# Seven products for eight in the first gate chunk, sums of w_down on Pool, gated loads, last store by ACT

## The chip, the cores and the metric

The kernel runs on one core of one Trainium2 chip. Times are device microseconds (us) of that core. The engines are PE (TensorE), PEld (its weight loads), DVE (VectorE), ACT (ScalarE), POOL (GpSimd, "Pool") and SP (SyncE, which only issues DMAs here). A traced execution has a "span" some 2 us shorter than the timed one. Traces are compared by spans, kernels by times. A single run of a one-core program has no known state, and is called a single run below.

## The reference, cut to what matters

```python
def _B_ref(x, w_gate, w_up, w_down):                 # x: 2048 x 448, F = 1792
    return (_gelu(x @ w_gate) * (x @ w_up)) @ w_down
x = A_x
xn = _layernorm(x)
s = attention(xn, k_cache, v_cache, wq, wo)          # 16 heads of 256, the last 512 keys  (cut)
g = silu(_B_ref(xn, w_gate, w_up, w_down))
return x + s * g
```

The 2048 rows go in four chunks of 512. The gate of a chunk is one matrix product with `w_down` (1792 x 448) after the gelu and the multiplication.

## The kernel before: the parts that matter

The program is a list of operations. Each goes to the in-order queue of one engine, and a semaphore wait is put in wherever an operation needs another engine's result. So an operation that is late makes everything behind it on its engine late (in experiment 12 a dead VectorE subtraction of 5.72 us made the multiplication behind it 5.07 us late).

TensorE forms gate and up for 128 columns at a time (a "unit"), two units per "pair", 28 pairs for the four chunks. After each unit ACT takes the gelu and VectorE multiplies:

```python
def gu_evac(n, b):
    act(gl[:, s, :], bank[b], ACT.Gelu_apprx_tanh, ...)
    o = actTh if c else actT                 # first chunk: bf16; later ones: f16
    K.op("dve", lambda e: e.tensor_tensor(o[:, c % 2, f, :], bank[b + 1], gl[:, s, :], ALU.mult), ...)
```

The pair after next fills the same banks again, so TensorE stops if VectorE is late with a multiplication (6.0 us of such waits in the trace of the changed kernel).

The product with `w_down` exists in two forms. `down` is the plain one, for the first chunk: 4 row tiles x 14 matmuls of 448 columns in bf16. `down7` cuts both operands in 2 x 2 blocks and needs seven block products for eight, in f16, for sums of activations (`sum_act`) and of weights (`sum_wd`) formed beforehand:

```python
def sum_wd(o, x, y):                         # 128 x 1568, f16
    add("dve", wdt[o][0], wdt[x][0], wdt[y][0], ..., ALU.subtract)
def sum_act(c, k, i=None):                   # 128 x 1024 or 128 x 768, f16
    ...
    add("dve", S(j)[0], x, y, bx + by, S(j)[1], op)
...
for n in range(4, NU, 2):                    # one unit pair
    gu_group((n, n + 1), cur)
    gu_evac(n, cur[0]); ln_b(); gu_evac(n + 1, cur[1])     # ln_b: normalisation of one tile of 128 rows
    if ln_t[0] < 8 or n >= 12: ln_a()                      # ln_a: its statistics, on VectorE and Pool
    ...                                                    # casts, sums: some per pair
    if n + 1 in DOWN_AT:                                   # {NF + 5: 0, 39: 1}
        ...                                                # down(0) after pair 18, down7(1) after pair 38
```

Attention follows: scores, softmax, a DMA transpose of the softmax weights (`pT<-pn`, 128 of them), the product with V, and `w_o`. Some gates of g and rows of x are loaded again through Pool's DMA queue.

The softmax here doesn't subtract the row's maximum and nothing guards it: scores larger than these inputs give would overflow.

## Time and profile before

| | before |
|---|---|
| time, first three runs | 543.99 us (543.13 to 544.43) |
| traced span | 541.5 us |
| PE / DVE / ACT / POOL busy | 535.7 / 376.3 / 313.4 / 39.5 us |
| mean granted TensorE clock | 0.999 |

TensorE is busy for 99% of the span, so it is the bound, and VectorE for 69%. The lines of the profile are in the prediction.

### The profile page before, as it was taken

What the parts mean: (1) busy time and instruction counts of PE and PEld (TensorE: products, weight loads), DVE (VectorE), ACT (ScalarE), POOL (GpSimd) and SP (SyncE); (2) the same over time, 40 slices, a digit from 0 to 9 for tenths busy, and PEclk for the clock granted to TensorE, in tenths of its full rate; (3) what the DMA queues carried; (4) which work ended last, traced back from release to release, by engine and by line L of the source; (5) the groups of instructions that cost most, each with busy time, mean ns of one, the idle gap of its engine ahead of it and who ended that gap; (6) DMA issues with size and microseconds to landing.
All of it is one profiled execution on the core that took longest, in us unless ns stands there. A gap on an engine that the chain in (4) does not pass through costs nothing.

```text
span 541.5 us, 10848 instructions
## 1 busy us (share of the span) xinstructions
PE 535.7 (99%) x4138; PEld 306.3 (57%) x4138; DVE 376.3 (69%) x825; ACT 313.4 (58%) x780; POOL 39.5 (7%) x78
## 2 busy tenths in 40 slices
PE   8999999999999999999999999999999999999997
PEld 5554457449644444884444469544444984444587
DVE  6673885799767757934875786467667934776775
ACT  5433854873667858206875860388488216876820
POOL 1130400000002000003001000120100003001010
PEclk9999999999999999999999999999999999999999
DMA  9569261921487767302781670066457402873731
GB/s 298 120 186 130 45 142 41 301 64 42 113 189 159 157 145 149 77 1 69 164 156 45 148 146 1 18 142 153 96 105 150 67 1 72 167 151 82 135 71 35
DMA packets 171604, 61.38 MB, mean 113 GB/s; under 512 B 155104, under 2 KB 168416, under 8 KB 171552
## 3 DMA queue, kind: packets, MB, share of 16 engines
q1 hardware_dynamic: 167776, 51.39, 43.7%
q0 software_dynamic: 3008, 8.72, 6.9%
q8 instruction: 33, 0.54, 0.4%
q10 hardware_dynamic: 768, 0.57, 0.3%
q14 instruction: 19, 0.16, 0.1%
HBM read 19.76 MB, written 3.67 MB: 43 GB/s over the span
## 4 chain that ended last, share of the span: by engine, by line
PE 97%; DMA 1%; DVE 0%; issue 0%; ACT 0%; ACTq 0%
PE bank L392 97%; DMA pT<-pn 1%; DMA x<-in_A_x_dram 0%; DVE stats L439 0%; PE bank L490 0%; DVE xn L465 0%; DVE mv L442 0%; ACT p L844 0%; PE bank L509 0%; DVE xnT L898 0%; DVE xnT L386 0%; DVE rstd L459 0%; ACTq L155 0%
## 5 line engine op out<-in xcount | busy, mean ns | idle before, releaser
L844 ACT ACTIVATE p<-bank 128x512 f32<-128x512 f32 x256 | 150.6, 596 | 28.2 <-DVE pn L851 26.4
L392 PE MATMUL bank<-pT,va 128*128 128x512 bf16 x512 | 120.8, 379 | 1.0 <-DMA pT<-pn 1.0
L392 PE MATMUL bank<-kT,qT 128*128 128x512 bf16 x512 | 121.0, 379 | 0.0
L851 DVE TENSOR_SCALAR pn<-p,rden 128x512 bf16<-128x512 f32 x256 | 113.0, 484 | 8.2 <-DMA pT<-pn 3.9
L392 PE MATMUL bank<-xnT,wq 64*128 64x512 bf16 x768 | 94.9, 376 | 0.0
L392 PEld LDWEIGHTS bank<-pT,va 128*128 128x128 bf16 x512 | 49.9, 98 | 61.5 <-DMA pT<-pn 2.2
L392 PEld LDWEIGHTS bank<-kT,qT 128*128 128x128 bf16 x512 | 49.4, 98 | 61.7 <-issue 3.4
L392 PE MATMUL bank<-xnT,wgu 64*128 64x512 bf16 (+2 forms) x768 | 83.9, 350 | 0.1
L383 ACT ACTIVATE qT<-bank 128x512 bf16<-128x512 f32 x76 | 44.1, 596 | 51.9 <-PE bank L392 50.3
L829 DVE CAST qT<-bank 128x512 bf16<-128x512 f32 x52 | 34.9, 690 | 49.6 <-PE bank L392 49.6
L392 PEld LDWEIGHTS bank<-xnT,wq 64*128 64x128 bf16 x768 | 36.7, 94 | 46.3 <-ACT p L844 2.1
L392 PEld LDWEIGHTS bank<-xnT,wgu 64*128 64x128 bf16 x768 | 36.9, 94 | 36.8 <-issue 0.6
L848 DVE RECIPROCAL rden<-rsum 128x2 f32<-128x2 f32 x128 | 21.2, 165 | 47.4 <-ACT p L844 47.2
L844 ACT ACTIVATION_READ_ACCUMULATOR p<-bank 128x1 f32 x256 | 51.6, 202 | 0.0
L392 PE MATMUL bank<-wt,sr 128*128 128x224 f16 x512 | 50.0, 259 | 0.0
L383 ACT ACTIVATE gl<-bank 128x512 bf16<-128x512 f32 x56 | 33.1, 596 | 28.5 <-PE bank L392 26.1
L392 PEld LDWEIGHTS bank<-wt,sr 128*128 128x128 f16 x512 | 49.0, 98 | 0.4 <-ACT oTh L383 0.2
L869 DVE TENSOR_SCALAR oTh<-bank 128x512 f16<-128x512 f32 x62 | 42.4, 684 | 0.0
L383 ACT ACTIVATE oTh<-bank 128x512 f16<-128x512 f32 x66 | 38.9, 590 | 4.1 <-PE bank L392 4.1
L392 PE MATMUL bank<-wt,oTh 128*128 128x224 f16 (+1 forms) x416 | 38.4, 252 | 0.0
L392 PEld LDWEIGHTS bank<-wt,oTh 128*128 128x128 f16 x416 | 37.2, 98 | 0.9
L377 POOL DMA_DIRECT2D g<-g_all x14 | 7.8, 556 | 379.9 <-DVE xnT L386 285.0
(82 smaller groups left out, 403.7 us busy)
## 6 DMA issues: line engine op xcount, KB each, us to landing
wtb<-in_A_wo_dram POOLq DMA_DIRECT2D x4, 896.0 KB, 10.4
wq<-in_A_wq_dram SPq DMA_DIRECT2D x2, 1536.0 KB, 7.2
va<-in_A_v_cache_dram SPq DMA_DIRECT2D x8, 256.0 KB, 5.2
pT<-pn SPq DMA_TRANSPOSE x128, 2.7
xr<-in_A_x_dram POOLq DMA_DIRECT2D x15, 112.0 KB, 2.4
wd<-in_B_w_down_dram SPq DMA_DIRECT2D x1, 1568.0 KB, 7.9
g<-g_all POOLq DMA_DIRECT2D x14, 112.0 KB, 2.3
out_dram<-xr POOLq DMA_DIRECT2D x12, 112.0 KB, 2.2
```

Of the source, the lines that this page charges most:

```text
L377: K.op(q, lambda e, o=o, i=i: e.dma_start(o, i), reads, writes, dma=True)
L383: K.op("act", lambda e, o=o, i=i: e.activation(o, i, func, scale=scale), reads, writes)
L392: ins = e.matmul(o, lhsT=l, rhs=r, start=st, stop=sp, skip_group_check=True)
L829: K.op("dve", lambda v, s=s, b=b: v.tensor_copy(qT[:, s, 1, :], bank[b + 1]), (b_ps[b + 1],), (b_qT[s][1],))
L844: K.op("act", lambda e, b=b, r=r, z=z: e.activation(p32[:, z, :], bank[b], ACT.Exp, scale=att_scale, accum_out=rsum[:, r:r + 1]), (b_ps[b] ...
L848: K.op("dve", lambda e, r=r: e.reciprocal(rden[:, r - 1:r + 1], rsum[:, r - 1:r + 1]), b_rsum[r - 1:r + 1], b_rden[r - 1:r + 1])
L851: K.op("dve", lambda e, r=r - 1 + t, z=(n - 1 + t) % NP32, y=y, t=t: e.tensor_scalar(pn[:, y, t, :], p32[:, z, :], rden[:, r:r + 1], None, ...
L869: K.op("dve", lambda v, i=i, b=b: v.tensor_scalar(oTh[:, i, :], bank[b], WS, None, op0=ALU.mult), (b_ps[b],), (b_oT[i],))
```

## The change

The intent is to save TensorE time in the first chunk (98 half-width matmuls for 56), to give Pool, idle for 93% of the span, the sums of weights, to move layer norms out of the pairs in which these sums run, and to remove two small waits in attention and at the end.

```diff
+        dn[0] = (dict(dn[1][0]),) + dn[1][1:]              # same places for the sums of chunk 0
-            o = actTh if c else actT                       # gu_evac: f16 always
-        def down(c, pairs): ...                            (removed)
         def sum_wd(o, x, y):
-            add("dve", wdt[o][0], wdt[x][0], wdt[y][0], ..., ALU.subtract)
+            add("pool", wdt[o][0], wdt[x][0], wdt[y][0], ..., ALU.subtract)
-        WD_CASTS = [(20, ...                               # casts of w_down by ACT
+        WD_CASTS = [(16, ...
-        DN_SUMS = [(24, sum_act, (1, k, 0)) ...] + [(30, sum_wd, x) ...] + [(34, sum_act, (1, k, 1)) ...]
+        WD_SUMS = [(20, (4, 4, 0)), (22, (5, 2, 4)), (22, (6, 5, 0)), (24, (3, 1, 5))]
+        ACT_SUMS = [(n, (c, k, i)) for c, i, ns in ((0, 0, (10, 10, 20, 20)), (0, 1, (22, 22, 24, 24)), ...
-        DOWN_AT = {NF + 5: 0, 39: 1}
+        DOWN_AT = {27: 0, 39: 1}
-            if ln_t[0] < 8 or n >= 12:
+            if ln_t[0] < 8 or 12 <= n and ln_t[0] < 12 or n >= 28:
+                def norms():                               # two layer norms, within down7 of chunk 0
+                    for f in (ln_a, ln_a, ln_b, ln_b): f()
-            dma("sp", out_view[:, t, c0:c1], ...)          # last_end
+            dma("sp" if c1 < N2 else "act", out_view[:, t, c0:c1], ...)
+                        now = [[o for o in K.ops if o.eng == "pe"][-1]]
-                            load_g2(t)                     # and the loads of xr likewise
+                            load_g2(t, now)                # not before TensorE has come to this place
... (cuts within and between the parts)
```

More of the change, by code (lines that the diff above doesn't have):

```diff
@@ L334, in bass_recurrent_scan__sliding_block_cached__geglu_ffn__prompt_kernel @@
                         [a_wq + 3 * SD + (3 + i) * CD for i in range(2)])}
+        dn[0] = (dict(dn[1][0]),) + dn[1][1:]
+        dn[0][0][3] = (actTh[:, 0, 0:NH, HC:QC], b_actT[0][0:NH])
         NPT, NPN, NP32 = 3, 3, 3
@@ L373, in qs, with dma @@
             return n - g + (QS - Q0 if g == 0 else 0)
-        def dma(q, o, i, reads=(), writes=()):
-            K.op(q, lambda e, o=o, i=i: e.dma_start(o, i), reads, writes, dma=True)
+        def dma(q, o, i, reads=(), writes=(), after=()):
+            K.op(q, lambda e, o=o, i=i: e.dma_start(o, i), reads, writes, dma=True, after=after)
         def dma_t(o, i, reads=(), writes=()):
@@ L557, in gu_evac @@
             act(gl[:, s, :], bank[b], ACT.Gelu_apprx_tanh, (b_ps[b],), (b_gl[s],))
-            o = actTh if c else actT
-            K.op("dve", lambda e: e.tensor_tensor(o[:, c % 2, f, :], bank[b + 1], gl[:, s, :], ALU.mult),
+            K.op("dve", lambda e: e.tensor_tensor(actTh[:, c % 2, f, :], bank[b + 1], gl[:, s, :], ALU.mult),
                  (b_ps[b + 1], b_gl[s]), (b_actT[c % 2][f],))
-        def down(c, pairs):
-            for t4 in range(4):
-                t = c * 4 + t4
-                b = bk(pairs, t4)
-                mms([(bank[b][:, 0:D], actT[:, c % 2, f, t4 * P:(t4 + 1) * P], wd[:, f, :], f == 0, f == NF - 1)
-                     for f in range(NF)], [b_wd] + b_actT[c % 2], (b_ps[b],))
-                s = t % 2
-                act(tmp[:, s, 0:D], bank[b][:, 0:D], ACT.Tanh, (b_ps[b],), (b_tmp[s],), scale=0.5)
-                K.op("dve", lambda e, t4=t4, b=b, s=s: e.scalar_tensor_tensor(
-                    out=g2w[t4 // 2][:, t4 % 2, :], in0=tmp[:, s, 0:D], scalar=1.0, in1=bank[b][:, 0:D],
-                    op0=ALU.add, op1=ALU.mult), (b_tmp[s], b_ps[b]), (b_g2w[t4],))
-                dma("sp", g2d[t], g2w[t4 // 2][:, t4 % 2, :], (b_g2w[t4],), (b_g2d[t],))
         def cast_wd(j, e, n, i):
@@ L581, in sum_wd @@
         def sum_wd(o, x, y):
-            add("dve", wdt[o][0], wdt[x][0], wdt[y][0], [wdt[x][1], wdt[y][1]], [wdt[o][1]], ALU.subtract)
+            add("pool", wdt[o][0], wdt[x][0], wdt[y][0], [wdt[x][1], wdt[y][1]], [wdt[o][1]], ALU.subtract)
         def sum_act(c, k, i=None):
@@ L750, in bass_recurrent_scan__sliding_block_cached__geglu_ffn__prompt_kernel @@
             (48, (o, x, y, i)) for i in range(NB) for o, x, y in ((5, 2, 4), (6, 5, 0), (3, 1, 5))]
-        WD_CASTS = [(20, (j, e, n, i)) for j, e, n in ((0, 0, 0), (4, 0, 1), (2, 1, 1), (1, 1, 0)) for i in range(2)]
-        DN_SUMS = [(24, sum_act, (1, k, 0)) for k in range(4)] + [
-            (30, sum_wd, x) for x in ((4, 4, 0), (5, 2, 4), (6, 5, 0), (3, 1, 5))] + [(34, sum_act, (1, k, 1)) for k in range(4)]
-        DOWN_AT = {NF + 5: 0, 39: 1}
+        WD_CASTS = [(16, (j, e, n, i)) for j, e, n in ((0, 0, 0), (4, 0, 1), (2, 1, 1), (1, 1, 0)) for i in range(2)]
+        WD_SUMS = [(20, (4, 4, 0)), (22, (5, 2, 4)), (22, (6, 5, 0)), (24, (3, 1, 5))]
+        ACT_SUMS = [(n, (c, k, i)) for c, i, ns in ((0, 0, (10, 10, 20, 20)), (0, 1, (22, 22, 24, 24)),
+                                                    (1, 0, (30, 32, 34, 34)), (1, 1, (36, 36, 38, 38)))
+                    for k, n in enumerate(ns)]
+        DOWN_AT = {27: 0, 39: 1}
         gu_evac(0, 0)
@@ L780, in bass_recurrent_scan__sliding_block_cached__geglu_ffn__prompt_kernel @@
                 load_wt(1, 1, 0)
-            for i in range(2 if n >= 24 else 1):
+            for i in range(2):
                 if WD_CASTS and n >= WD_CASTS[0][0]:
                     cast_wd(*WD_CASTS.pop(0)[1])
-            for i in range(2 if n in (30, 32, 34, 36) else 1):
-                if DN_SUMS and n >= DN_SUMS[0][0]:
-                    _, f, x = DN_SUMS.pop(0)
-                    f(*x)
+            while WD_SUMS and n >= WD_SUMS[0][0]:
+                sum_wd(*WD_SUMS.pop(0)[1])
+            while ACT_SUMS and n >= ACT_SUMS[0][0]:
+                sum_act(*ACT_SUMS.pop(0)[1])
             for i in range(2 if n >= 40 else 1):
@@ L794, in bass_recurrent_scan__sliding_block_cached__geglu_ffn__prompt_kernel @@
             if n + 1 in DOWN_AT:
-                assert not DN_SUMS or DN_SUMS[0][0] > n, DN_SUMS
-                if DOWN_AT[n + 1] == 1:
-                    end = down7(1, (cur[0], cur[0] + 1, cur[1], cur[1] + 1, nxt[0], nxt[0] + 1),
-                          (g2x[:, 0:2, :], g2x[:, 2:4, :]), b_g2x)
-                    end(0, 1)
-                    end(2, 3)
-                    cur, nxt = (nxt[1], cur[1]), (cur[0], nxt[0])
-                else:
-                    down(DOWN_AT[n + 1], cur)
-                    cur, nxt = nxt, cur
-                    K.reuse([wdt[j][1] for j in (0, 1, 2, 4)])
+                def norms():
+                    for f in (ln_a, ln_a, ln_b, ln_b):
+                        f()
+                end = down7(DOWN_AT[n + 1], (cur[0], cur[0] + 1, cur[1], cur[1] + 1, nxt[0], nxt[0] + 1),
+                            (g2x[:, 0:2, :], g2x[:, 2:4, :]), b_g2x, then=norms if n < 28 else None)
+                end(0, 1)
+                end(2, 3)
+                cur, nxt = (nxt[1], cur[1]), (cur[0], nxt[0])
                 if DOWN_AT[n + 1] == 1:
@@ L873, in bass_recurrent_scan__sliding_block_cached__geglu_ffn__prompt_kernel, with load_g2 @@
         o_view = oTh.rearrange("p (h e) (r q) -> p e r h q", e=2, r=2)
-        def load_g2(t):
-            dma("pool", g2[:, t % NG2, :], g2d[t], (b_g2d[t],), (b_g2[t % NG2],))
+        def load_g2(t, after=()):
+            dma("pool", g2[:, t % NG2, :], g2d[t], (b_g2d[t],), (b_g2[t % NG2],), after)
         def burst_end(t, ns=(0, 1)):
@@ L900, in last_end @@
             add("dve", xs[:, t4, c0:c1], xs[:, t4, c0:c1], x[:, c0:c1], by + bx, by)
-            dma("sp", out_view[:, t, c0:c1], xs[:, t4, c0:c1], by, ())
+            dma("sp" if c1 < N2 else "act", out_view[:, t, c0:c1], xs[:, t4, c0:c1], by, ())
         def burst(c):
@@ L1035, in bass_recurrent_scan__sliding_block_cached__geglu_ffn__prompt_kernel @@
                             load_v(g)
+                        now = [[o for o in K.ops if o.eng == "pe"][-1]]
                         for t in range(NG2):
-                            load_g2(t)
+                            load_g2(t, now)
                         for t in range(NXR):
-                            dma("pool", xr[:, t, :], x_view[:, t, :], (), b_xr[t])
+                            dma("pool", xr[:, t, :], x_view[:, t, :], (), b_xr[t], now)
                     if end and p:
```

## The prediction

> **What bounds the kernel now.** I read the page's busy table and the slices first, then the chain that ended last, then the waits of TensorE, then the timelines of TensorE, Pool and the store queue in the stretches that the change touches.
>
> ```profile
> PE 535.7 (99%) x4138; PEld 306.3 (57%) x4138; DVE 376.3 (69%) x825; ACT 313.4 (58%) x780; POOL 39.5 (7%) x78
> PE 97%; DMA 1%; DVE 0%; issue 0%; ACT 0%; ACTq 0%
> ```
>
> TensorE (PE) works 535.7 of 541.5 us at the full granted clock, and 97% of the chain that ended last is its matmuls. So only three things can move the time: less TensorE work, fewer TensorE waits, a shorter tail. The waits of TensorE are three lines in all:
>
> ```profile
> PE bank L509 <- DVE epst L423: 1.2, 1, 1.2
> PE bank L392 <- DMA pT<-pn: 1.0, 1, 1.0
> PE bank L490 <- DVE xn L465: 0.4, 1, 0.4
> ```
>
> The first and third are the start, which the change leaves alone. The second is one wait inside attention, at 170 us; the chain in order of time shows it:
>
> ```profile
> 164.73 5.29 DMA pT<-pn
> 170.02 0.05 issue
> 170.07 368.31 PE bank L392 x2592
> ```
>
> One transpose of softmax weights took 5.29 us to land, where the page's list of DMA issues has 2.7 us as the median of these 128. Beside it the Pool timeline has this:
>
> ```profile
> 162.59 1.32 POOL L377 DMA_DIRECT2D g<-g_all  x2 [94.99 <-DVE rden L848]
> 163.90 1.59 POOL L377 DMA_DIRECT2D xr<-in_A_x_dram  x3
> ```
>
> Five loads of 112 KB each, issued just before that transpose. These are the loads the change gates.
>
> [...] a VectorE sum ran from 60.42 to 61.08, and the small Pool operation that began at 60.59 took 0.56 us, to 61.15, where its like at 57.57 took 0.22:
>
> ```profile
> 57.57 0.22 POOL L449 TENSOR_SCALAR ve<-mv 128x1 f32<-128x1 f32 x1 [2.15 <-DVE mv L442]
> 60.59 0.56 POOL L449 TENSOR_SCALAR ve<-mv 128x1 f32<-128x1 f32 x1 [2.15 <-DVE mv L442]
> ```
>
> [...]
>
> **The change, part by part.**
>
> *Seven products for eight, first chunk.* The old form and the form that the second chunk already uses stand in the TensorE timeline:
>
> ```profile
> 37.92 10.77 PE L392 MATMUL bank<-wd,actT 128*128 128x448 bf16 x56
> 48.62 0.82 PE L392 MATMUL bank<-xnT,wgu 64*128 64x512 bf16 x6
> ...
> 78.94 1.51 PE L392 MATMUL bank<-wdh,actTh 128*128 128x224 f16 x14
> ...
> 88.44 0.82 PE L392 MATMUL bank<-xnT,wgu 64*128 64x512 bf16 x6
> ```
>
> Start to start, the old form takes 48.62 - 37.92 = 10.70 us (56 x 191 ns), the new one 88.44 - 78.94 = 9.50 us (98 x 96.9 ns). Saved on the path: **1.20 us**. The products move from after unit pair 18 to after unit pair 26, which costs TensorE nothing.
>
> *Sums of activations.* Eight more on VectorE: four of 1024 elements at 0.66 to 0.68 us and four of 768 at 0.55 us, together 4.9 us. One pair of units lasts 3.02 us (gelus start at 34.35 and 37.37). In the pairs 20 to 26 VectorE has two multiplications, about 1.3 us, and, as the layer norms are moved out, at most 1.3 us of sums (pair 20 also still has one normalisation, 0.6 us): 3.2 us in pair 20, 2.4 us in 22 and 24. Nothing is lost, if these run at their present durations.
>
> *Sums of w_down to Pool.* VectorE is freed of four of 1568 elements, 0.96 to 0.97 us each, 3.9 us in all; off the path before, so no gain. On Pool they get a deadline. The products now start at 37.92 + 4 x 3.02 = 50.0 us. The first product (9.50/7 = 1.36 us) needs no sum; the second, from 51.36 us, reads the sum that Pool forms last. Pool can start when its last reciprocal root is done, 41.42 + 0.57 = 42.0 us (the casts on ACT are done earlier: after the gelus of pair 18 at 38.5, plus 1.74 us, so 40.3). So it has **9.36 us for four sums, 2.34 us each.** [...]
>
> *Layer norms of two tiles within the products.* About 2.9 us of VectorE (twice 0.62 + 0.18 for the statistics, 0.6 for the normalisation) at the start of a 9.5 us stage in which VectorE otherwise waits (3.6 us for TensorE before its first combination in the second chunk). Hidden, though their Pool steps queue behind the sums.
>
> *Gated loads.* Five loads leave 162.6 us and are issued after the first query projection of the next group, about 192 us. The transposes at 163 to 170 us keep the engines to themselves, so the wait of **1.03 us** should go. At 192 us they meet two K transposes and three V loads; the DMA is already about full from 193 to 199 us. 0.56 MB at some 250 GB/s adds an estimated 2.2 us there. K must be there at 198.3, the first V at 200.1 us; the V loads are issued at 194.1 us and take 4.4 us, so land at about 199. There is 1 to 2 us of slack: a stall of 0 to 1 us is possible.
>
> *Last store by ACT.* The store queue's timeline around the three last stores:
>
> ```profile
> 537.67 0.33 SPq L377 DMA_DIRECT2D out_dram<-xnT  x1
> 538.16 1.17 SPq L377 DMA_DIRECT2D out_dram<-xnT  x1
> ```
>
> The second issue held the queue until 539.33, while the last result was ready at 538.71 + 0.22 = 538.93. From ACT's own queue it can go at once: **0.4 us** off the tail.
>
> *Sum.* 543.99 - 1.20 - 1.03 - 0.4 = 541.4 us, before whatever Pool costs.
>
> **The rivals.**
> *A: Pool is in time.* Speaking for it is the shape of the change: casts are moved four units earlier, layer norms are moved out of exactly the pairs in which Pool sums, and the products are put off to pair 26. That looks like a schedule fitted to a slow Pool. Time: 541.2 to 541.8 us.
> *B: Pool is late.* The sums end after 51.36 us and a new wait of TensorE for Pool takes the place of what was saved. [...]
> *C: Pool locks out VectorE.* The six activation sums in pairs 20 to 24 each wait for a Pool sum, and Pool for them (six times 0.6 us, 3.7 us more for Pool at worst). VectorE's multiplications queue behind. A bank pair filled by one unit pair is needed again 3.02 us after that pair ends, and the second multiplication ends 1.9 us after it (24.08 + 0.69 against 22.85), so VectorE can be late by about 1 us before TensorE stops. [...]
> *D: gated loads come late for V.* Up to 1 us, 542.4 us.
>
> **Range and chances.** I give A about 50%, a stall of 0.5 to 3 us (fast C, mild B, D) 30%, a larger one 20%. The median lies a little above A's: **542.2 us**. The low end is A less some run spread (the three runs before spread 1.3 us): 540.8. The high end is B at full size with part of C: 547.3. Faster by over 2% would be below 533.1, which no term reaches: 0.01. Slower by over 2%, above 554.9, needs more than the worst of C: 0.02. Within 2%: 0.97.
>
> **What would show it right or wrong.** The matmuls of the first chunk's products should span 9.5 us; if they do, step one holds. A line of TensorE waiting for Pool in its waits, or for VectorE in pairs 24 to 28, shows B or C; the duration of the 1568-element Pool operation decides between them and A (under 2.3 us: A). VectorE sums far above 0.68 us, ending with a Pool sum, show C. The wait for the transpose at 170 us should be gone, the transposes' longest landing nearer 3 us; a new wait at 198 to 201 us shows D. The last store should be issued by ACT at about half a microsecond after the last matmul. A time below 540 us would mean that I missed a gain; above 548 us, that Pool and VectorE block each other at full size.

Sum of the parts: 541.4 us before whatever Pool costs. To it B added a wait of TensorE for Pool at two paces, for 545.8 and 542.8 us, and C a stall by lateness and by the lock, for 549 us, or about 1 us of stall with a faster Pool; Pool's pace in them was estimate or assumption. The high end of 547.3 us is B's 545.8 with part of C and rests on the same estimate. The "some 250 GB/s" is an estimate beside the trace's 214 GB/s from 193 to 199 us, with 287 in its fullest microsecond, and the "full" of the DMA there is a busy share of 0.94.

## The result, and the profile after

| | before | after |
|---|---|---|
| median of four runs each | 543.56 us | 550.77 us (550.45 to 550.86) |
| traced span | 541.5 us | 548.9 us |
| mean granted TensorE clock | 0.999 | 0.994 |

The ratio is 1.013, with a 95% interval of 1.0112 to 1.0147. A ratio here is the mean time of one kernel's fast runs over that of the other's of the same rounds, so not quite the ratio of the medians quoted. The kernel became slower by 1.3%, inside the class "within 2%" but outside the predicted range of 540.8 to 547.3 us.

From the page of the kernel after: busy time by engine, two rows of the 40 slices (tenths; the clock row shows 9 for full), and the chain that ended last.

```profile
PE 535.5 (98%) x4155; PEld 311.0 (57%) x4180; DVE 390.3 (71%) x835; ACT 314.2 (57%) x782; POOL 52.4 (10%) x82
...
PE   9995999999999999999999999999999999999998
...
PEclk9998899999999999999999999999999999999999
...
PE 89%; DVE 4%; ACT 3%; DMA 2%; issue 1%; ACTq 0%; DVEq 0%
```

VectorE is now 4% of the chain, where it was 0%. TensorE is busy for only five tenths of the fourth slice (a slice is 13.7 us, so this is 41 to 55 us), and the clock was below full there and in the next (8 tenths in both). That is where Pool's sums run. The waits of TensorE (what it waited for: us in total, times, longest) begin with

```profile
PE bank L394 <- DVE actTh L560: 6.0, 2, 4.8
...
PE bank L394 <- DMA pT<-pn: 1.1, 1, 1.1
```

The first line is new: TensorE waits for VectorE's multiplications, not for Pool. Two more lines of that list, for `qT` and for "issue", are no waits: this trace has 487 of 512 matmul records of the scores, and the holes are counted as idle.

The timelines say why (start, duration, engine, line, operation, output and inputs). Pool after the change:

```profile
41.95 3.15 POOL L388 TENSOR_TENSOR wdh<-wdh 128x1568 f16<-128x1568 f16 x1
45.26 3.21 POOL L388 TENSOR_TENSOR wdt<-wdh 128x1568 f16<-128x1568 f16 x1
48.54 3.47 POOL L388 TENSOR_TENSOR wdt<-wdt,wdh 128x1568 f16<-128x1568 f16 x1
51.98 3.59 POOL L388 TENSOR_TENSOR wdt<-wdh,wdt 128x1568 f16<-128x1568 f16 x1
```

VectorE in the same stretch:

```profile
42.09 3.36 DVE L467 TENSOR_SCALAR xn<-x,mv,rstd 128x448 bf16<-128x448 bf16 x2 [0.31 <-POOL rstd L453]
45.37 0.68 DVE L560 TENSOR_TENSOR actTh<-bank,gl 128x512 f16<-128x512 f32 x1
45.97 3.04 DVE L388 TENSOR_TENSOR sd<-sd,actTh 128x1024 f16<-128x1024 f16 x1
48.94 3.62 DVE L388 TENSOR_TENSOR sd<-actTh,sd 128x1024 f16<-128x1024 f16 x1
...
53.68 2.30 DVE L388 TENSOR_TENSOR actTh<-actTh 128x768 f16<-128x768 f16 x1
56.02 0.56 DVE L388 TENSOR_TENSOR sd<-actTh 128x768 f16<-128x768 f16 x1
```

And the same normalisation in the kernel before:

```profile
39.07 0.61 DVE L465 TENSOR_SCALAR xn<-x,mv,rstd 128x448 bf16<-128x448 bf16 x2 [0.31 <-POOL rstd L451]
```

Read the ends against each other. Pool's sums end at 45.10, 48.47, 52.01 and 55.57 us. VectorE's normalisation ends at 45.45, its sums at 49.01, 52.56 and 55.98: each about half a microsecond after a Pool sum, which is what is left to do once Pool lets go. The sums that start after Pool is done take 0.55 to 0.56 us. (A normalisation is two instructions, of 448 and of 64 elements, shown as one line.) The multiplication at 45.37, one of whose inputs comes from a bank, ran its 0.68 us beside a Pool sum undisturbed. Against the undisturbed durations VectorE was held for (3.36 - 0.61) + (3.04 - 0.68) + (3.62 - 0.68) + (2.30 - 0.55) = 9.8 us.

The windows of the same stretch (length, busy time of PE, PEld, DVE, ACT and POOL with instruction counts, clock, DMA share, GB/s):

```profile
48.50:53.20 4.70, 0.00 (x0) 0.00 (x0) 4.70 (x4) 0.01 (x1) 4.66 (x2) 0.75 0.24 32
53.20:58.50 5.30, 5.28 (x28) 1.87 (x28) 5.27 (x7) 1.06 (x2) 2.37 (x1) 0.58 0.00 0
58.50:68.00 9.50, 9.50 (x100) 9.31 (x98) 7.73 (x17) 1.28 (x3) 1.57 (x4) 1.00 0.13 29
```

In the first TensorE does nothing for 4.7 us while VectorE and Pool are both "busy". In the second it works through one unit pair at a mean granted clock of 0.58 (0.50 from 51 to 57 us, so it fell while TensorE still stood), in 58.51 - 53.22 = 5.29 us where a pair takes 3.02. The third is the seven products: 9.50 us, as predicted, at full clock.

Behind that, the gated loads left only after TensorE's first query matmuls, as meant, and one transpose in a later chunk was late:

```profile
198.77 1.10 POOL L379 DMA_DIRECT2D g<-g_all  x2 [118.16 <-PE bank L394]
```

```profile
427.91 1.90 PE L394 MATMUL bank<-pT,va 128*128 128x512 bf16 x8 [1.08 <-DMA pT<-pn]
```

**Where the 7.4 us of span come from.** I laid the two traces side by side at fixed places of the program:

| place | before | after | difference |
|---|---|---|---|
| start of unit pair 28 | 60.71 | 68.01 | +7.3 |
| first query projection | 112.62 | 119.93 | +7.3 |
| query projection behind the late transpose of 170 us | 189.17 | 195.27 | +6.1 |
| a later query projection | 280.56 | 286.94 | +6.4 |
| a product with `w_o` | 421.71 | 429.65 | +7.9 |
| last products with `w_o` | 519.27 | 527.21 | +7.9 |
| end of span | 541.5 | 548.9 | +7.4 |

(In the timeline of the kernel before, pair 28 begins inside a merged line; its start is that of pair 26, 57.69, and the 3.02 us of a pair: 60.71.) The +7.3 of the first row are waits of 1.22 and 4.78 us, 2.27 us of slow pair, 0.24 us left over, less the 1.20 us of the products. The gated loads then take 1.2 us off, late transposes add 1.8 us, and the tail gives 0.5 us back.

### The profile page after: what moved, and what is told of

The parts are those of the page before. It is cut to its first block, busy times and chain, and to the rows that moved or that the text cites. A ratio compares the mean times of both kernels' runs of the same rounds, so it can differ in the third digit from the quotient of the medians.

```text
span 548.9 us, 10923 instructions
## 1 busy us (share of the span) xinstructions
PE 535.5 (98%) x4155; PEld 311.0 (57%) x4180; DVE 390.3 (71%) x835; ACT 314.2 (57%) x782; POOL 52.4 (10%) x82
## 4 chain that ended last, share of the span: by engine, by line
PE 89%; DVE 4%; ACT 3%; DMA 2%; issue 1%; ACTq 0%; DVEq 0%
PE bank L394 88%; DMA pT<-pn 2%; ACT p L830 2%; DVE pn L837 1%; DVE sd L388 1%; PE bank L511 1%; DVE rden L834 0%; DVE actTh L560 0%; ACT qT L385 0%; PE bank L492 0%; ACT gl L385 0%; DVE oTh L855 0%; ACT oTh L385 0%; DVE xn L467 0%; DVE xnT L884 0%
## 5 line engine op out<-in xcount | busy, mean ns | idle before, releaser
L394 PE MATMUL bank<-kT,qT 128*128 128x512 bf16 x487 | 117.8, 379 | 2.3 <-ACT qT L385 1.0
L394 PE MATMUL bank<-xnT,wgu 64*128 64x512 bf16 (+2 forms) x768 | 85.9, 355 | 6.1 <-DVE actTh L560 6.0
L560 DVE TENSOR_TENSOR actTh<-bank,gl 128x512 f16<-128x512 f32 x56 | 37.4, 687 | 11.9 <-PE bank L394 6.2
```

The lines of the kernel that those rows point to most:

```text
L394: ins = e.matmul(o, lhsT=l, rhs=r, start=st, stop=sp, skip_group_check=True)
L560: K.op("dve", lambda e: e.tensor_tensor(actTh[:, c % 2, f, :], bank[b + 1], gl[:, s, :], ALU.mult), (b_ps[b + 1], b_gl[s]), (b_actT[c % 2] ...
```

## The experiments

The theory: **the lock.** Pool's long sums and VectorE's normalisation and sums exclude each other instruction by instruction. VectorE's multiplications queue behind, and the stop that this makes in TensorE also lowers its clock. Rivals: **overload** (VectorE simply has too much to do in these pairs), **lateness** (what depends on Pool's results is late), and for the clock, **Pool itself** (activity of Pool, not the stop).

### 1. The sums of weights back on VectorE, all else as changed

```diff
         def sum_wd(o, x, y):
-            add("pool", wdt[o][0], ...
+            add("dve", wdt[o][0], ...
```

> The changed kernel with one word undone: the four sums of w_down on VectorE again, in the same places of the program. Theory (the lock): in the changed kernel the 1568-element Pool sums of 3.2 to 3.6 us held VectorE's fast and two-input operations, VectorE fell behind, TensorE waited 6.0 us for it and then ran slower matmuls. Without Pool sums VectorE has 3.9 us more work in these pairs but no operation above 1.1 us; TensorE waits at most 1 us there, the granted clock stays at full, about 542 us (541.3 to 542.8). Rival 1 (VectorE simply has too much work with the eight added activation sums): with 3.9 us more on it this must be slower than the changed kernel, above 551 us. Rival 2 (TensorE needs the sum that Pool forms last): also repaired here, about 542 us; this run does not tell it from the lock.

Measured: 541.89 us (541.34 to 542.09, five runs), 0.9981 of the kernel before [0.9967, 0.9994]; span 539.7 us, clock 1.0. VectorE's timeline:

```profile
42.10 0.61 DVE L467 TENSOR_SCALAR xn<-x,mv,rstd 128x448 bf16<-128x448 bf16 x2 [0.30 <-POOL rstd L453]
...
43.22 0.96 DVE L388 TENSOR_TENSOR wdh<-wdh 128x1568 f16<-128x1568 f16 x1
44.10 0.68 DVE L388 TENSOR_TENSOR sd<-sd,actTh 128x1024 f16<-128x1024 f16 x1
```

With 3.9 us more work VectorE is done earlier: every operation has its own duration again, and the only wait of TensorE in the stretch is 0.15 us before a product. Overload falls. One word of the change costs 548.9 - 539.7 = 9.2 us of span.

### 2. The same, with the sums spread over later pairs and the products in another order

```diff
-        WD_SUMS = [(20, (4, 4, 0)), (22, (5, 2, 4)), (22, (6, 5, 0)), (24, (3, 1, 5))]
+        WD_SUMS = [(22, (4, 4, 0)), (24, (5, 2, 4)), (24, (6, 5, 0)), (26, (3, 1, 5))]
-                end = down7(..., then=norms if n < 28 else None)
+                end = down7(..., (4, 6, 5, 3, 2, 1) if n < 28 else (3, 6, 5, 4, 2, 1), norms if n < 28 else None)
```

(on top of experiment 1)

> The changed kernel with the sums of w_down on VectorE, spread over unit pairs 22, 24, 24 and 26, and the products of the first chunk in the order 4, 6, 5, 3, 2, 1, so that each finds its sum ready. Theory: no wait of TensorE in the first chunk at all; 543.6 - 1.2 (products) - 1.2 (gated loads) - 0.5 (last store) = 540.7 us, plus up to 0.7 us of the small slips that the changed kernel shows inside attention: 540.6 to 541.6 us, faster than the kernel before. Rival (VectorE overloaded): a wait of TensorE for VectorE between 45 and 60 us, above 543 us.

Measured: 541.71 us (540.79 to 542.24, five runs), 0.9979 [0.9967, 0.9992]. No TensorE wait is left between 45 and 60 us, and the products run from 49.91 to 59.40. This version beats both kernels, by 0.2% over the first. The median is just outside what I expected. Against the kernel before it is 2.2 us ahead at 189 us and only 0.5 us at 519 us: late transposes (the longest waits are 0.48 us at 263 and 0.56 at 419) take 1.7 us back. More on these below.

### 3. Idle Pool subtractions beside the good version

Four subtractions of the same size on Pool whose result nobody reads, added to the version of experiment 2, at the place where the change starts its sums:

```diff
+            for i in range(4):
+                f = lambda e: e.tensor_tensor(scrt[:, 0:1568], wgu[:, 0, 0, 0:1568], wgu[:, 1, 0, 0:1568], ALU.subtract)
+                last = [K.op("pool", f, [b_wgu] + ..., (b_scr,), after=last)]
```

> The spread kernel plus four Pool subtractions of 1568 16-bit elements whose result nobody reads, issued where the changed kernel's Pool sums stand. No instruction waits for them by data, except the Pool steps of two layer norms queued behind them. Theory (the lock): VectorE's operations with two SBUF inputs and the fast normalisation are held up to 3.5 us each, TensorE waits for VectorE 4 to 9 us in all, 546 to 552 us. Rival 2 (what cost time was that TensorE's data came late from Pool): no data comes from Pool, so the time is that of the spread kernel, 541 us.

Measured: 553.09 us (single run; the kernel before beside it 542.84), correct. The four took 13.13 us; VectorE's normalisation beside them:

```profile
42.22 6.26 DVE L467 TENSOR_SCALAR xn<-x,mv,rstd 128x448 bf16<-128x448 bf16 x2 [0.30 <-POOL rstd L453]
```

The next two sums took 3.21 and 3.62 us, TensorE waited 7.0 us for multiplications (4.12 and 2.84, each followed by a slow pair), and the products began at 62.05 us instead of 49.91. No data comes from these Pool operations (only the small steps of two layer norms stand behind them in Pool's queue), so lateness of Pool's results is not needed for the loss. The normalisation, which ended only at 48.48, was held over two Pool operations and not one. The time is 1.1 us above what I expected, but not because of the waits, which lie within the 4 to 9 us: of the 12.14 us by which the products are late, some 5 us are not waits but slow matmuls (granted clock 0.50 from 48 to 58.5 us and 0.57 from there to 62), which the expectation did not have.

### 4. Pool's sums in the kernel before

```diff
         def sum_wd(o, x, y):
-            add("dve", wdt[o][0], ...
+            add("pool", wdt[o][0], ...
```

> The kernel before with one word changed: the four sums of w_down for the second chunk on Pool. Theory (the lock): Pool starts at about 68 us, [...]each sum takes 3.2 us or more, VectorE's activation sums at 74 to 81 us (0.55 us each) are held to 1 to 3.5 us, and the products, from 80.3 us on, wait for VectorE or for the last Pool sum (ready at about 81.5 to 83): 1 to 4 us slower than before, 545 to 548 us. Rival 1 (overload of VectorE): VectorE has 3.9 us less to do, so the time is that of before, 543.5 us, or less.

Measured: 549.49 us (single run; before 542.84). Pool's sums ran from 64.99 to 78.60 (expected from about 68; Pool's issues of two `w_o` loads, at 65.12 to 67.59 in the kernel before, came behind them here, at 78.56), in time for the product that needs them at 83.76. VectorE's operations beside them were held as in the change: the normalisation took 3.35 us, two sums 3.04 and 2.44.

```profile
64.99 3.15 POOL L386 TENSOR_TENSOR wdh<-wdh 128x1568 f16<-128x1568 f16 x1
```

```profile
65.13 3.35 DVE L465 TENSOR_SCALAR xn<-x,mv,rstd 128x448 bf16<-128x448 bf16 x2 [0.24 <-POOL rstd L451]
```

TensorE waited 3.1 us for multiplications in three pieces of at most 1.5 us, the second chunk's products were 3.46 us late, and the clock stayed at 0.999. The rest of the loss, to 5.9 us at the last products with `w_o` (525.15 for 519.27), is mostly late transposes: waits of 1.49 us (1.03 in the kernel before) and 1.72 us. The result was 1.5 us over my expected range, for that reason. So the lock needs nothing else of the change, and stops of up to 1.5 us did not lower the clock.

### 5. Idle Pool writes instead of reads

```diff
-                f = lambda e: e.tensor_tensor(scrt[:, 0:1568], wgu[:, 0, 0, 0:1568], ...
+                f = lambda e: e.memset(scrt[:, 0:5120], 0.0)
```

(in the place of experiment 3's subtractions)

> The spread kernel plus four Pool memsets of 5120 16-bit elements into dead memory at the same place: Pool busy for several us (estimate 3 to 4 us each, from the 0.20 us of a memset of 128 against 0.10 of one of 1 in the trace), but it reads nothing from SBUF. If what excludes the engines is the read side, [...]VectorE's sums keep their 0.55 to 0.68 us and only the fast normalisation with one input may be held: below 543 us. If any long Pool operation holds VectorE (write side too): 546 us or more, as with the reads.

Measured: 550.87 us (single run; before 543.44). Neither branch of the expectation came out whole: the two-input sums were not held by the memsets (as I read it below), which was to mean a time below 543 us, and yet it cost as much as the change (1.16 us of it by a late load of V, see experiments 7, 8 and 10). Pool and VectorE:

```profile
41.77 17.64 POOL L592 MEMSET scr<- 128x5120 bf16 x4
```

```profile
41.93 8.67 DVE L467 TENSOR_SCALAR xn<-x,mv,rstd 128x448 bf16<-128x448 bf16 x2 [0.31 <-POOL rstd L453]
...
46.99 3.62 DVE L388 TENSOR_TENSOR sd<-sd,actTh 128x1024 f16<-128x1024 f16 x1
...
56.53 0.96 DVE L388 TENSOR_TENSOR wdt<-wdh 128x1568 f16<-128x1568 f16 x1
```

Here one has to read closely. A memset takes 17.64 / 4 = 4.4 us, and the four last until 59.41. The normalisation was held over two of them, to 50.60, and TensorE stopped for 6.0 us. The sum at 46.99 looks held too. But six operations behind the normalisation, multiplications and sums, are on record from 46.38 on, mostly 0.6 us apart as usual, and all of them end with it at 50.60 or 50.61. I read this as waiting for the normalisation, not for the memset: the two-input sum at 56.53, in the middle of the fourth memset and with no normalisation before it, ran its normal 0.96 us, and so did the three sums after it (0.97, 0.55 and 0.55). So two kinds of VectorE work were shut out by different things in these runs: two-input sums by Pool operations that read (2.30 to 3.62 us for 0.55 to 0.68 in the change) but not by memsets (0.55 to 0.97 us, as alone), the one-input normalisation by both (3.36 us for 0.61 in the change, 8.67 here). The prediction counted only the sums, and that the read side would decide was the assumption.

### 6. Pool's sums cut in sevenths

```diff
-            add("pool", wdt[o][0], wdt[x][0], wdt[y][0], ...
+            for k in range(NH):
+                add("pool", wdt[o][0][:, k, :], wdt[x][0][:, k, :], wdt[y][0][:, k, :], ...
```

> The changed kernel with each Pool sum cut into seven of 224 elements. Theory (the lock is held for one instruction): no VectorE operation is held by more than one piece at a time, about 0.5 us, so no VectorE sum exceeds about 1.3 us and TensorE's wait for VectorE at 45 to 53 us falls below 1 us. Pool itself still takes 13 to 17 us from 42 us on, so the last sum comes at 56 to 60 us and TensorE now waits for Pool at its second product, from 51.4 us, by 4 to 8 us: total 544 to 551 us, with the wait under another name. If the lock were not per instruction, VectorE's operations stay at 3 us and TensorE still waits for VectorE first.

Measured: 552.3 us (single run; before 543.44). VectorE is free again: the normalisation takes 1.19 us, the sums 0.54 to 1.09, and no wait for VectorE is left. A VectorE operation now loses at most about the length of one short Pool operation (0.58 us of the normalisation's 1.19; a piece took 0.57 to 0.81 us on average). But the 28 pieces last until 60.54 us, 18.6 us in all where 13 to 17 were expected, and the waits of TensorE show what stood behind:

```profile
PE bank L394 <- POOL wdt L388: 9.2, 1, 9.2
```

So the exclusion is per instruction: in pieces of Pool's work the normalisation lost 0.58 us, beside a whole sum 2.75. It also shows the prediction's rival B, Pool's lateness, which the change itself hides: its own products began only at 58.51, and the one that needs Pool's last sum at 59.86, after that sum's end at 55.57.

### 7, 8 and 10. The small parts alone, on the kernel before

```diff
+                        now = [[o for o in K.ops if o.eng == "pe"][-1]]
-                            load_g2(t)             (xr likewise)
+                            load_g2(t, now)
```

> The kernel before with the gated loads alone. The wait of TensorE for the transpose at 170 us should go, the projection that follows should begin 1.0 to 1.2 us earlier (189.17 before), no new wait at 198 to 201 us: 542.4 us, 1.0 to 1.2 us less than before. Rival: the loads only move their collision to the K and V loads at 192 us, time as before.

```diff
-            dma("sp", out_view[:, t, c0:c1], ...)
+            dma("sp" if c1 < N2 else "act", out_view[:, t, c0:c1], ...)
```

> The kernel before with the last stores on the ACT queue alone. From the last matmul group's end to the end of the span before took 3.1 us, in the changed kernel 2.6: 0.4 to 0.6 us less than before, 543.0 us. Rival: the end is set by the landing of a store that no queue shortens, no difference.

Both edits together:

> The kernel before with the gated loads and the ACT store, without the seven products: the two parts that paid by themselves. If the parts add and TensorE's instruction count (which is that of before here) decides where its fetches meet transposes: 1.0 + 0.5 us less than before, 541.5 to 542.2 us, no wait for a transpose above 0.3 us after 200 us. Rival: the gain of gating is lost again by other late transposes, 542.5 us or more.

| | time (median, runs) | ratio to before |
|---|---|---|
| gated loads | 542.44 us (6) | 0.9982 [0.9965, 0.9999] |
| last store by ACT | 542.64 us (5) | 0.9981 [0.9967, 0.9995] |
| both | 542.30 us (6) | 0.9978 [0.9964, 0.9992] |

Gated, the wait for the transpose at 170 us is gone, 1.02 us are gained at 189 us (188.15 for 189.17), and there is no wait at 198 to 201 us. So rival D did not come about here, nor in the changed kernel. It is not impossible: of the nine traces with gated loads, that of experiment 5 has a wait for V. There the V loads landed 7.1 to 7.3 us after their issue, where they take 4.2 to 4.6 us in the kernel before (4.9 to 7.0 in the changed one):

```profile
207.51 1.90 PE L394 MATMUL bank<-pT,va 128*128 128x512 bf16 x8 [1.16 <-DMA va<-in_A_v_cache_dram]
```

The store's gain varies. From the last VectorE operation to the end of the span it took about 2.4 to 2.9 us in the five traces with all stores on SP's queue (2.6 in the kernel before). With ACT's queue it took 2.0 to 2.1 us in eight of nine traces, the changed kernel among them, but 2.6 with both parts. So it is mostly worth 0.3 to 0.8 us and was once worth nothing, and the 0.8 us between the medians of the store alone hold more than the store: that traced run also has a transpose wait of 0.78 us in place of 1.03. The parts do not add: both together are no faster, within the intervals, than either alone, and just outside the 541.5 to 542.2 us that I expected.

### 9. Moving instruction fetches

The late transposes needed a cause. In the DMA records of the kernel before there is a small queue that carries instructions: the page lists it as "q8 instruction", 33 packets of 16 KB in the run, which has 8276 TensorE instructions (matmuls and weight loads), so one to every 251 of them; each took about 1.1 us on one of the 16 DMA engines (0.4% of the 16 engines' span). A second queue, "q14 instruction", has 19 smaller packets. I sorted the 128 transposes by what lay beside them between issue and landing:

| beside the transpose | before: number, mean, longest | after: number, mean, longest |
|---|---|---|
| no fetch, no load through Pool's queue | 75, 2.74, 2.87 us | 83, 2.74, 2.86 us |
| an instruction fetch (q8 or q14) | 39, 3.57, 4.64 us | 36, 3.58, 5.29 us |

(In the kernel before the other 14 lay beside Pool's loads: mean 3.46 us, with the 5.29 us of the prediction's chain among them; after, the other 9.) Of the 39, the 22 beside a packet of q8 took 3.95 us on average, up to 4.64, and the 17 beside q14 alone 3.06, up to 3.66. Every transpose without company landed within 2.87 us. The change adds 42 matmuls and 42 weight loads, and later packets come at other places of the schedule: the one at 203.2 us in the kernel before came at 205.6, 2.4 us later, where the schedule is some 6 us later. To shift them by another means, I cut the warm-up matmuls in more and smaller ones, on the version of experiment 2:

```diff
-        warm(9, 2, QC)
+        warm(36, 2, 96)
```

> The spread kernel with the nine warm-up matmuls of 512 columns at the start replaced by 36 of 96 columns: 27 matmuls and 27 weight loads more, so TensorE's instruction stream, which the trace shows to be fetched in packets of 16 KB about every 256 instructions, is fetched at other places of the attention stage. In the spread kernel two transposes beside such packets, near 258 and 413 us, landed after 4.7 us and made TensorE wait 0.5 and 0.6 us. Theory (the fetch phase decides it): these two waits move or go; the time changes by up to 1.5 us either way, 540.3 to 542.5 us, and transposes that overlap no fetch still land within 3.0 us. Rival (the late transposes belong to fixed places of the schedule, for instance the end of a chunk): the waits stay near 258 and 413 us, time as the spread kernel.

Measured: 542.62 us (541.51 to 543.22), 0.998 of before [0.9964, 0.9996]. The median is 0.1 us outside the expected range. The new warm-up itself lost 1.06 us (the products began at 50.97 for 49.91). The wait at 263 us was gone, the one at 419 us stayed (0.45 us, now at 416, with fetch packets beside it again), and one of 0.18 us was new at 172. So theory and rival each got one of the two waits. All seven traces with the first chunk's seven products have a wait at this last place, to within one group of eight matmuls (0.13 to 1.08 us), and none of the seven others has one, so the rival of fixed places is not excluded. The association with the fetches is strong in every trace; that they cause the waits is not shown.

### 11 and 12. A VectorE delay without Pool

Does the clock fall because of Pool, or because TensorE stops? One dead VectorE subtraction was put behind pair 22 of the kernel before, in two lengths:

```diff
+            if n == 22:
+                add("dve", delt[:, :, :], wgu[:, 0, 0:2, :], wgu[:, 1, 0:2, :], ..., ALU.subtract)    # 3584 elements; 12: 0:3, 5376
```

> The kernel before with one dead VectorE subtraction of 3584 elements (about 3.9 us) after unit pair 22, and nothing on Pool: VectorE is late as in the changed kernel, without any lock. TensorE waits for VectorE by an estimated 2 to 3 us. Theory of the clock (a long enough stop of TensorE lowers the granted clock for some us): at this length perhaps not yet; the time lost equals the wait to within 0.3 us if the clock stays at full, and exceeds it if not. 546 to 547 us.

> The same with 5376 elements (about 5.8 us): TensorE waits an estimated 4 to 5 us, as in the changed kernel (4.8). Theory of the clock: the granted clock falls to about 0.8 in the slice after it, the next unit pair takes about 5.3 us in place of 3.0, and the time lost exceeds the wait by about 2.2 us: 549.5 to 551 us. Rival (the slow pair in the changed kernel was due to Pool, not to the stop): lost time equals the wait, 547.5 to 549 us.

Measured (single runs; before 543.58): 546.20 us with a delay of 3.86 us and 548.22 with 5.72. The shorter made four waits of TensorE, 1.8 us together, the longest 1.04, and the clock stayed at 1.00; the products were 2.46 us late. The longer made one, and then a slow pair:

```profile
63.76 1.46 PE L392 MATMUL bank<-xnT,wgu 64*128 64x512 bf16 x6 [2.90 <-DVE actTh L559]
```

```profile
62.00:66.00 4.00, 2.24 (x12) 0.81 (x14) 3.73 (x8) 2.20 (x3) 1.77 (x3) 0.72 0.06 13
```

Six matmuls took 1.46 us where they take 0.81; the stretch of 16 matmuls from 63.76 to 67.15 took 3.39 us where it takes 1.72, so 1.67 us were lost to the clock (granted 0.50 in this stretch, 1.00 before and after it). The second chunk's products were 4.72 us late: 2.90 of wait, 1.67 of clock, and about 0.16 left over (the shorter delay has some 0.16 for each of its four waits too); what it is, the traces do not show. Here Pool does none of the long sums and the clock fell to 0.50 all the same, behind the stop of 2.90 us, so they are not needed for it. The lock shows from its other side: a Pool operation that takes 0.22 us alone was held for 5.63 us beside the longer subtraction. Both waits were shorter than I had expected (1.8 for 2 to 3 us, 2.9 for 4 to 5). The multiplication behind the delay came 3.20 and 5.07 us late, and TensorE waited 1.04 and 2.90 us for it, so VectorE has about 2.2 us of slack there, more than I took. The time of the longer was below my range for that reason.

## Why the prediction was wrong, point by point

**The bound and the saving were right.** TensorE bounds the kernel, and the seven products take 9.50 us as worked out. The 1.20 us are there: the good version of experiment 2 is 1.30 us ahead of the kernel before at 112 us.

**The step that failed is in the part on sums of activations: "Nothing is lost, if these run at their present durations."** They did not. Beside Pool's sums they took 2.3 to 3.6 us for 0.55 to 0.68. The condition was named, and the text even showed a VectorE sum holding up a Pool operation. The trace of the kernel before also has the other direction, which was overlooked: a normalisation at 35.66 took 1.20 us for 0.61, until the first of two DMA issues of Pool (35.49 to 36.88) was done. But the sum of the parts was made as though the condition held, and "before whatever Pool costs" then left the largest term to the rivals.

**Rival C had the mechanism, and its sum had the wrong terms.** It made 549 us out of Pool's lateness, at the estimate of Pool's pace, and 3.7 us of Pool being held. Measured, Pool was held for 0.8 us only (its four sums took 13.42 us, where four times 3.15 is 12.6), and its lateness was not paid, as the products came later anyhow. In their place stood 6.0 us of TensorE waiting for VectorE, and 2.3 us of clock, a term that no rival had. The one-input normalisation, which C did not count as lockable, was alone held for 2.75 us. The near agreement (549 against 550.77) is thus partly luck.

**Pool's speed** was an estimate that no trace showed. Measured, a sum took 3.15 us at its fastest, 2.0 ns per element, where the prediction allowed 2.34 us. With that, rival A (in time, under 2.3 us) was dead before any lock. **"That looks like a schedule fitted to a slow Pool"** gave A 50%: the shape of a change shows what its author meant, not that it fits.

**The gated loads were right** (1.02 to 1.2 us for a predicted 1.03; no wait for V in the change, one in the nine traces with them). **The store was right in kind**, mostly 0.3 to 0.8 us for a predicted 0.4. **The layer norms within the products** cost nothing: no wait of TensorE is between 58.5 and 68 us. (Their sum is a little off: twice 0.62 + 0.18 + 0.6 is 2.8 us, not 2.9.) **What no step had** is that later transposes come late at other places, 1.8 us here; the same term took back 1.7 us in the good version.

**What stays open**: whether the instruction fetches cause the late transposes or only accompany them, and so whether a phase of the instruction stream exists in which the whole 2.6 us of the change's useful parts survive to the end.

## What to carry to other kernels

Before work is moved to Pool, list which VectorE operations run beside it: in these runs those with two SBUF inputs waited for whole Pool instructions that read, and the one-input normalisation also for those that only write, so a Pool operation of 3 us added up to 3 us to the next 0.6 us VectorE operation (3.62 us for 0.68 beside Pool sums of 3.47 and 3.59) and to everything queued behind. Cutting Pool's work in small instructions freed VectorE but made Pool slower (18.6 us for 13.4), so an idle Pool is not spare VectorE time. Stops of TensorE of 2.90 and 4.78 us were paid again in clock here (1.67 and 2.27 us), those of up to 1.5 us were not, and a small gain early in a tight schedule was lost again to late transposes (1.7 us of the good version's 2.2), so compare places along the trace and not the end alone.
